# Gated attention followed by a Hyena-style gate: six PSUM banks become one pool, and score runs take two or three units

## The chip, the cores and the metric

The kernel runs on one core of one Trainium2 chip. The metric is the time on the device in microseconds (us), the median of several executions. Besides, one execution is recorded by the hardware profiler; its trace gives the start and duration of each instruction and what each engine waited for. Below, PE is TensorE (matmuls), PEld its weight loads, ACT is ScalarE, DVE is VectorE, POOL is GpSimd and SP is SyncE, which issues most DMAs.

## The reference, cut to what matters

```python
B, S, D = 8, 3136, 256          # d_qk = 64
scores = (z @ z.transpose(0, 2, 1)) / S
attn   = np.maximum(scores, 0.0) ** 2
x      = u * (attn @ v)                       # gated attention
proj   = x @ w_proj                           # D -> 3 D
x1, x2, x3 = proj[..., :D], proj[..., D:2*D], proj[..., 2*D:]
X2 = np.fft.rfft(x2, n=S, axis=1)
H  = np.fft.rfft(filter_fft, n=S, axis=0)[None]
y  = x1 * np.fft.irfft(X2 * H, n=S, axis=1) * x3
out = y @ w_out
```

The inputs and the output are float32. The matmuls run in bfloat16 and accumulate in float32.

## The kernel before, in words

**Scores and weighing.** A batch entry has 3136 positions, cut into 25 tiles of 128 (the last has 64 rows) on one side and into seven chunks of 512, 512, 512, 512, 512, 256 and 320 columns on the other. A *unit* is a chunk with two tiles (with up to four of a narrow chunk). For each unit PE multiplies z with itself: matmuls of 64 rows (line 1352), two at a time, one in the upper and one in the lower half of the array, since d_qk is 64. Their result fills a pair of PSUM banks. ACT takes the relu of the pair (line 1527, tile R), DVE or ACT squares it (1536 or 1534, tile A, eight buffers), and PE weighs v with it (1382, all 128 rows), adding up in two further banks, one for each half of D (`ps_o`). As scores are symmetric, part of the units is not computed again: a DMA transpose (1467) mirrors A tiles into M tiles, which are weighed for later chunks. The last, 64-row tile is weighed separately (1489, `weigh_short`), tacked on to a later score group, `DELAY` groups on. When a chunk is complete, DVE multiplies with u (1577, two results xT).

**All the rest.** From xT PE computes the three projections (901, 913, 946), and a discrete Fourier transform in two steps of small matmuls forwards (758, then 819 and 811), the product with the filter on DVE (1019), and the same backwards (827 and 811, then 1109), then the output matmul (1140). Each of these writes one PSUM bank, which ACT or DVE evicts. Intermediate spectra go through DRAM.

**The order** is made while the program is built. A planner (class `Plan`) holds tasks with an assumed cost on each engine and due times of DMAs, keeps a queue for each kind of PE task and lists for the other engines, and fixes each engine's instruction order. On PE the kinds are S (scores), W (weighing), and FA, FB, FZ (the rest). S comes first whenever it can start within 0.04 us. Whether W or the others come next is set by a credit, which grows by `PACE` with every W and falls with the cost of the others. A task is ready when its inputs and its buffers (`takes`, classes `Slots`) are. The planner adds 0.11 us whenever PE changes between S and any other kind. `Plan.pick` gives a task that both ACT and DVE can do to the second one if it would be done earlier there. On the chip the engines follow the fixed order and wait on semaphores.

**PSUM** has eight banks in the kernel before:

```python
ps_s = Pool("ps_s", 2, [P, 2, 512], F32, PS)          # two pairs, for scores
ps_o = [Pool(f"ps_o{dh}", 1, [P, 512], F32, PS) for dh in range(2)]
ps_m = Pool("ps_m", 2, [P, 512], F32, PS)             # all other matmuls
groups = [scored[i : i + 2] for i in range(0, len(scored), 2)]
```

An S task is a group of two units and takes both pairs of `ps_s`. When no W is left, at the end of the kernel, other matmuls may also use a bank of each `ps_s` pair and the `ps_o` banks (`Plan.choice`, `plan.spare`).

Of the kernel before, what the change touches and what calls it, by code (L numbers as in the profile page):

```python
# [25 lines left out]
HOLD = 3  # L26
DELAY = 2
LATE_PUT, LATE_LOAD, LATE_TURN, LATE_C, LATE_D2 = 3.0, 1.0, 1.5, 2.5, 1.0
# [3 lines left out]
FINAL = (0, 2, 4, 6, 1, 3, 5)  # L32
ZP, ZL = 0, 0.0
REACH = 2
INF = float("inf")
# [7 lines left out]
def c_dve(n):  # L43
    return 0.068 + n * 0.00104
# [14 lines left out]
class Slots:  # L59
# [4 lines left out]

    def take(self):
        self.taken += 1
        self.freed.append(None)
        return self.taken - 1

    def when(self, ahead=0):  # L70
        i = self.taken + ahead - self.n
        if i < 0:
            return 0.0
        if i >= len(self.freed) or self.freed[i] is None:
            return INF
        return self.freed[i]


# [23 lines left out]
class Plan:  # L102


    def __init__(self):
        self.free = {e: 0.0 for e in ("PE", "ACT", "DVE", "SP", "POOL")}
        self.queues = {"S": [], "W": [], "FA": [], "FB": [], "FZ": []}
        self.pend = {e: [] for e in ("ACT", "DVE", "SP", "POOL")}
        self.credit = 0.0
        self.mode = None  # L110
        self.n = 0
        self.spare = []
        self.bus = 0.0

# [30 lines left out]
    def run(self, task, engine, start):  # L145
        takes = [self.choice(s) for s in task.takes]
        self.bank = takes[0] if takes else None
        task.slots = [(s, s.take()) for s in takes]
# [12 lines left out]
        for t, i in task.frees:  # L161
            s, k = t.slots[i]
            if i == 0 and getattr(t, "holders", 1) > 1:
                t.holders -= 1
                t.held_to = max(getattr(t, "held_to", 0.0), end + lat)
                continue
            s.freed[k] = max(getattr(t, "held_to", 0.0), end + lat) if i == 0 else end + lat
        for kid in task.kids:
            for d, extra in kid.deps:
                if d is task:  # L170
                    kid.ready = max(kid.ready, end if extra == ISSUED else end + lat + (extra or 0.0))
            kid.left -= 1
            if not kid.left and kid.kind is None:
                self.offer(kid)

    def pick_pe(self):
        t = self.free["PE"]
        got = {}
        for k, window in (("S", 1), ("W", 1), ("FA", 6), ("FB", 6), ("FZ", 6)):
            best = None  # L180
            for task in self.queues[k][:window]:
                s = max(t, self.ready_at(task))
                if s < INF and (best is None or s < best[0] - 1e-9):
                    best = (s, task)
            if best:
                got[k] = best
        if not got:
            return None
        near = t + 0.04
# [56 lines left out]
def kernel(  # L246
# [85 lines left out]
    o_p = Pool("ost", 2, [P, 4, D], F32)  # L332
    ps_s = Pool("ps_s", 2, [P, 2, 512], F32, PS)
    ps_o = [Pool(f"ps_o{dh}", 1, [P, 512], F32, PS) for dh in range(2)]
    ps_m = Pool("ps_m", 2, [P, 512], F32, PS)

    plan.spare = [ps_m.slots, ps_s.slots, *(p.slots for p in ps_o)]

    def bank(dtype=F32):
        if plan.bank is ps_s.slots:  # L340
            return ps_s.tile()[:, 0, :]
        for p in ps_o:
            if plan.bank is p.slots:
                return p.tile()
        return ps_m.tile([P, 512], F32) if dtype == F32 else ps_m.tile([P, 1024], BF16)

# [5 lines left out]
    def pe(kind, emit, cost, deps=(), takes=(), **kw):  # L352
        return job(kind, lambda e: emit(), {"PE": cost}, deps, takes, **kw)
# [169 lines left out]
    for i, (t0, t1) in enumerate(zip(z_cuts, z_cuts[1:])):  # L523
        step_ = -(-(t1 - t0) // -(-(t1 - t0) // 8))
        for g0 in range(t0, t1, step_):
# [31 lines left out]

            tt = pe("FA", turn, c_pe(*[P] * nt), [(c0, 0.22), (c1, 0.22)], takes=[ps_m.slots])
            tt.frees.append((c0, 0))
# [108 lines left out]

    t4_t = pe("FB", t4_pe, 0.06, [t1_done], takes=[ps_m.slots])
    t4_done = on("DVE", t4_copy, 0.35, [t4_t])  # L670
# [42 lines left out]
    for i0 in range(0, NS, 8):  # L713
# [11 lines left out]

        tt = pe("FB", turn, c_pe(*[P] * n), [s2_done[-1]], takes=[ps_m.slots])
        tb = job(None, back, {"DVE": c_dve2(n * KR)}, [tt], prio=3)
# [23 lines left out]
    def dft1(kind, get, t0, nt, dst, deps, free=None, late=0.0):  # L751
# [14 lines left out]

        a = pe(kind, mm, c_pe(n), deps, [ps_m.slots, s1_p.slots])
        if free:
# [92 lines left out]
    for j0 in range(0, NJ, 4):  # L861
        ld, ibox = load_spec(DF, j0, 4, puts, LATE_F)
        for i in range(4):
# [9 lines left out]

            a = pe("FB", mm, c_line(j0 + i), [*s2_done, ld], [ps_m.slots])
            if i == 3:
# [9 lines left out]
    def add_proj(b, c, xt, xt_tasks):  # L885
# [7 lines left out]
        def to_gates():  # L893
            for nb in range(2):
# [27 lines left out]

                a = pe(kind, mm1, c_pe(cw, cw), xt_tasks, [ps_m.slots, x1_p.slots])
# [4 lines left out]
                a3 = pe(kind, mm3, c_pe(cw, cw), [*xt_tasks, a], [ps_m.slots, g_p.slots])  # L928
                e3 = on("DVE", ev3, c_dve(cw), [a3, e1], prio=late)
# [4 lines left out]
        def to_spectrum():  # L934
            t0, n = T0[c], len(tiles[c])
            at = 0
            while at < n:
# [15 lines left out]

                a = pe("FA", mm2, c_pe(*[D] * (2 * nt)), xt_tasks, [ps_m.slots, x2_p.slots])
                e2 = job(None, ev2, both(nt * D), [a])
# [18 lines left out]
    def add_spectrum(b, puts):  # L974
# [7 lines left out]
        for g in range(NJ // 2):  # L982
# [9 lines left out]
            for i in range(2):  # L992
# [12 lines left out]

                a = pe("FB", mm, c_line(j), [ld, *deps0, *firsts], [ps_m.slots, *([] if i else [xh.slots])])
                firsts = [a]
# [23 lines left out]
            def inv(g=g, xb=xb, z_=z_, a0=a0, gh=gh):  # L1031
# [3 lines left out]
                for i in range(2):  # L1035
# [17 lines left out]
                    a = pe(  # L1053
                        "FB", mm, c_line(j) * (1 + final), [z_, *gx["firsts"], *(minus_task if final else [])], [ps_m.slots] + ([gh.slots] if new else [])
                    )
# [29 lines left out]
    def add_end(b, lasts, gtasks, cs, kind="FB", src=c_p, dsts=(o_p,), late=0, behind=(), then=(), split=False, mids=(y_p,)):  # L1085
        for at, c in enumerate(cs):
# [7 lines left out]
            for dh in range(2):  # L1094
# [16 lines left out]
                def ev(dh=dh, c=c, w=w, box=box, yb=yb):  # L1111
# [3 lines left out]
                    kind, mm, c_pe(*[P] * nt), [ld, t4_done, *firsts, gtasks[2 * c + dh][1], *then],  # L1115
                    [ps_m.slots] + ([mid.slots] if dh == 0 else []),
                )
# [10 lines left out]
            for i0 in range(0, nt, 2):  # L1128
# [16 lines left out]
                def eo(e, i0=i0, n=n, last=last, box=box, ob=ob):  # L1145
# [9 lines left out]
                    kind, mo, c_pe(*[D] * (2 * n)), [*ys, *firsts],  # L1155
                    [ps_m.slots] + ([dst.slots] if i0 == 0 else []),
                )
# [184 lines left out]

    def score_mm(un):
        b, c, k = un
        cw = CHUNKS[c]
        ps = ps_s.tile()
        zt = zT[b]
# [43 lines left out]
    def add_weigh(un, data, done):  # L1391
        global_k = len(plans[un[:2]])

        def part(dhs):
            b, c, k = un
            cw = CHUNKS[c]
            n = sum(t < NT - 1 for t in plans[b, c][k][1])
# [3 lines left out]
                [ps_o[dh].slots for dh in dhs] if k == 0 else [],  # L1401
            )
            if b == 0 and c == 0:
                after(t, next(at for n_, at in V_AT if max(plans[b, c][k][1]) < n_))
# [71 lines left out]

    ends_at = {}
    for gi, g in enumerate(groups):
# [15 lines left out]
    for gi, g in enumerate(groups):  # L1494
# [12 lines left out]
        def sg(g=g, more=more):  # L1507
            for un in g:
                score_mm(un)
# [6 lines left out]
        tails[gi] = st  # L1516
        for i, un in enumerate(g):
            b, c, k = un
# [43 lines left out]
            if last:  # L1562
# [3 lines left out]
                for dh in range(2):  # L1566

                    def xe(dh=dh, b=b, c=c, cw=cw, xt=xt):
# [102 lines left out]
```

## Time and profile before

| | |
|---|---|
| median of 3 executions | 1018.22 us (1015.94 to 1019.5) |
| the profiled execution | 1017.51 us, of it the span from first to last instruction 1015.7 us |
| granted clock of TensorE, mean | 0.995 |
| busy: PE, ACT, DVE, POOL | 97%, 88%, 80%, 18% of the span |
| matmuls | 6046 |
| units scored (relu instructions, line 1527) | 528 |
| HBM read and written | 141 GB/s over the span |

A line of a group in the profile gives line, engine, operation, output and inputs by the program's names, shapes and count, then busy time and mean duration, then the engine's idle time just before. A line of the timeline gives start (us), duration (us), engine, line and operation, and in brackets an idle time before it. A line of the waits gives who waited for whom, total us, number of times and the longest. "issue" stands for time in which the engine waited for nothing that the profile shows. Matmuls overlap, so their durations add up to more than the time they take; the distance from start to start is the cost of one.

### The profile page before, as it was taken

How to read it: one execution, taken by the hardware profiler on the slowest of the kernel's cores; microseconds unless marked ns; L12 is line 12 of the kernel's file. 1: busy time of each engine (PE TensorE's matmuls, PEld its weight loads, DVE VectorE, ACT ScalarE, POOL GpSimd, SP SyncE). 2: the span in 40 equal slices, each digit the busy share in tenths (PEclk: the TensorE clock that was granted, in tenths of full speed). 3: DMA queues.
4: the chain of work that ended last, by engine and by line, in shares of the span. 5: the costliest groups of instructions: out<-in, count | busy, mean ns of one | idle time of the engine just before them, and what ended most of it. 6: DMA issues, size and time to landing. Idle time of an engine off the chain costs nothing.

```text
span 1015.7 us, 17732 instructions
## 1 busy us (share of the span) xinstructions
PE 989.6 (97%) x6046; PEld 483.1 (48%) x6046; DVE 812.8 (80%) x1469; ACT 892.0 (88%) x1218; POOL 186.7 (18%) x401
## 2 busy tenths in 40 slices
PE   6999999999999999999999999999999999999986
PEld 2344544455444554446444464444644455444664
DVE  7866688978889688987789778887798868896574
ACT  5988899988999799897999979998899979998774
POOL 5042301121012210213012131113201221000000
PEclk9999999999999999999999999999999999999989
DMA  9799769878986998898978779896899779968456
GB/s 166 135 172 171 143 128 176 164 145 172 210 176 126 164 205 192 153 158 149 226 159 151 142 159 217 159 177 141 167 208 175 148 137 198 215 145 170 110 184 208
DMA packets 331770, 170.18 MB, mean 168 GB/s; under 512 B 241160, under 2 KB 306504, under 8 KB 331680
## 3 DMA queue, kind: packets, MB, share of 16 engines
q1 hardware_dynamic: 303952, 138.09, 62.5%
q0 software_dynamic: 27728, 30.97, 21.0%
q8 instruction: 47, 0.77, 0.3%
q14 instruction: 43, 0.35, 0.1%
HBM read 90.26 MB, written 53.35 MB: 141 GB/s over the span
## 4 chain that ended last, share of the span: by engine, by line
PE 91%; DVE 4%; ACT 1%; issue 1%; DMA 1%; SPq 1%; ACTq 0%; DVEq 0%
PE ps_o_t L1382 48%; PE ps_s_t L1352 13%; PE ps_m_t L946 5%; PE ps_m_t L913 4%; PE ps_m_t L901 4%; PE ps_m_t L1140 4%; PE ps_m_t L758 3%; PE ps_m_t L819 3%; PE ps_m_t L827 3%; PE ps_m_t L1109 2%; PE ps_o_t L1489 1%; ACT R_t L1527 1%; DVE xT_t L1577 1%; PE ps_m_t L811 1%; DVE yT_t L1112 1%
## 5 line engine op out<-in xcount | busy, mean ns | idle before, releaser
L1527 ACT ACTIVATE R_t<-ps_s_t 128x1024 f32<-128x1024 f32 (+3 forms) x528 | 474.6, 939 | 40.9 <-PE ps_s_t L1352 30.5
L1382 PE MATMUL ps_o_t<-A_t,v_t 128*128 128x512 bf16 (+2 forms) x2016 | 458.3, 355 | 1.3 <-DMA un_t<-in_u_dram 0.7
L1382 PEld LDWEIGHTS <-v_t 128*128 128x128 bf16 x2688 | 254.0, 98 | 227.0 <-issue 27.5
L1536 DVE TENSOR_TENSOR A_t<-R_t 128x1024 bf16<-128x1024 f32 (+2 forms) x269 | 297.0, 1111 | 31.3 <-ACT R_t L1527 23.0
L1534 ACT ACTIVATE A_t<-R_t 128x1024 bf16<-128x1024 f32 (+4 forms) x259 | 247.9, 967 | 5.3 <-DMA M_t<-A_t 1.6
L1352 PE MATMUL ps_s_t<-zT_t 64*128 64x512 bf16 (+2 forms) x1064 | 153.8, 357 | 1.7 <-ACT R_t L1527 1.2
L410 POOL COPY tick<-xT_t 1x1 bf16<-1x1 bf16 x54 | 11.7, 217 | 731.9 <-DVE xT_t L1577 731.9
L1577 DVE SCALAR_TENSOR_TENSOR xT_t<-ps_o_t,uT_t 128x256 bf16<-128x256 f32 (+2 forms) x224 | 76.2, 382 | 35.6 <-PE ps_o_t L1382 29.9
L921 DVE TENSOR_TENSOR gate_t<-ps_m_t,x_t 128x256 bf16<-128x256 f32 (+2 forms) x208 | 68.9, 384 | 35.9 <-PE ps_m_t L913 22.2
L361 ACT ACTIVATE x_t<-ps_m_t 128x512 bf16<-128x512 f32 (+2 forms) x115 | 63.4, 573 | 24.9 <-PE ps_m_t L901 21.3
L1019 DVE TENSOR_TENSOR xh<-xh,H 100x1024 bf16<-100x1024 bf16 x120 | 81.1, 684 | 4.6 <-ACT xh L361 3.9
L1382 PE MATMUL ps_o_t<-M_t,v_t 128*128 128x512 bf16 (+2 forms) x352 | 82.0, 353 | 0.0
L1352 PEld LDWEIGHTS <-zT_t 64*128 64x128 bf16 x1064 | 34.4, 94 | 99.4 <-issue 96.8
L365 DVE CAST x_t<-ps_m_t 128x512 bf16<-128x512 f32 (+2 forms) x92 | 57.1, 636 | 12.8 <-PE ps_m_t L946 8.8
L1112 DVE TENSOR_TENSOR yT_t<-ps_m_t,gate_t 128x512 bf16<-128x512 f32 (+2 forms) x95 | 57.2, 617 | 12.3 <-PE ps_m_t L1109 11.1
L365 DVE CAST s_t<-ps_m_t 128x512 bf16<-128x512 f32 (+1 forms) x65 | 43.0, 668 | 23.4 <-PE ps_m_t L758 22.9
L401 POOL DMA_DIRECT2D un_t<-in_u_dram x112 | 59.9, 556 | 6.8 <-issue 5.5
L420 POOL DMA_DIRECT2D v_t<-in_v_dram x112 | 59.6, 554 | 5.7 <-issue 3.1
L946 PE MATMUL ps_m_t<-wp,xT_t 128*128 128x256 bf16 x394 | 57.4, 273 | 0.7 <-DVE gate_t L921 0.5
L901 PE MATMUL ps_m_t<-xT_t,wp 128*128 128x512 bf16 (+2 forms) x210 | 54.6, 355 | 1.5 <-DVE xT_t L1577 1.4
L1140 PE MATMUL ps_m_t<-wo,yT_t 128*128 128x256 bf16 (+1 forms) x344 | 52.4, 274 | 1.9 <-DVE yT_t L1112 1.6
L913 PE MATMUL ps_m_t<-xT_t,wp 128*128 128x512 bf16 (+2 forms) x208 | 52.7, 355 | 0.1
(196 smaller groups left out, 958.4 us busy)
## 6 DMA issues: line engine op xcount, KB each, us to landing
out_dram<-ost_t SPq DMA_DIRECT2D x66, 256.0 KB
spec<-s_t SPq DMA_DIRECT2D x96, 128.0 KB
spec_in_t<-spec SPq DMA_DIRECT2D x28, 392.0 KB
spec<-gs_t SPq DMA_DIRECT2D x28, 392.0 KB
v_t<-in_v_dram POOLq DMA_DIRECT2D x80, 128.0 KB, 3.7
un_t<-in_u_dram POOLq DMA_DIRECT2D x80, 128.0 KB, 4.8
conv_in_t<-spec SPq DMA_DIRECT2D x33, 256.0 KB
out_dram<-ost_t SPq DMA_DIRECT2D x19, 128.0 KB
```

The costliest lines, as they stand in the source:

```text
L365: nc.vector.tensor_copy(out_, in_)
L901: nc.tensor.matmul(box["p"][:, :cw], wp16[:, k, ds(nb * P, P)], xt["t"][:, k, :cw], start=(k == 0), stop=(k == 1),)
L913: nc.tensor.matmul(box["p3"][:, :cw], wp16[:, k, ds((4 + nb) * P, P)], xt["t"][:, k, :cw], start=(k == 0), stop=(k == 1),)
L946: nc.tensor.matmul(box["p"][:, ds(k_ * D, D)], xt["t"][:, k, ds((at + k_) * P, P)], wp16[:, k, ds(D, D)], start=(k == 0), stop=(k == 1),)
L1019: nc.vector.tensor_tensor(x[:, 1 - i], x[:, 0], h, ALU.mult)
L1140: nc.tensor.matmul(box["p"][:rows, ds(i * D, D)], yb["y"][:, k, ds((i0 + i) * P, rows)], wo16[:, k, :], start=(k == 0), stop=(k == 1),)
L1352: nc.tensor.matmul(blocks(ps, len(pair), cw)[:m, i], zt[h, ds(t * P, m)], zt[h, ds(C0[c], cw)], start=True, stop=True)
L1382: nc.tensor.matmul(o, row(v16[b], t)[:, ds(dh * P, P)], x, start=(k == 0 and i == 0), stop=(last and i == len(pair) - 1),)
L1527: nc.scalar.activation(blocks(box["R"], n, cw)[:rows], blocks(live[un], n, cw)[:rows], AF.Relu)
L1534: nc.scalar.activation(a, r, AF.Square)
L1536: nc.vector.tensor_tensor(a, r, r, ALU.mult)
L1577: nc.vector.scalar_tensor_tensor(x, f, inv_s2, ut, ALU.mult, ALU.mult)
```

## The change

The pools `ps_s` and `ps_m` become one store of six banks, three tiles of two banks each. `Pairs` gives out a whole tile to a score unit, and `Singles` one bank to any other matmul; a single is put beside one that is held longest, and at most `MOST = 3` singles are held at once. An S task is one unit (`GROUP = 1`). The planner decides when a run of S tasks starts: with more than `AMPLE` us of weighing queued (`backlog`) it wants three free pairs, otherwise two; until they are free, other tasks that can start earlier go first, the F kinds only with more than `BACKLOG` us queued. A run that has begun goes on as long as a pair is free within `STAY` us. Further: the F kinds go ahead of W only when less than `FULL` us of work is queued on ACT and DVE; the second engine is charged (`YIELD`) for tasks that only it can do and that would be held up; `DELAY` goes from 2 groups of two to 4 groups of one; and the second xT evaluation counts as ready when the first is issued, not when it has ended.

```diff
-DELAY = 2
+DELAY = 4
+GROUP = 1
+BACKLOG, AMPLE, STAY = 2.0, 4.0, 0.1
+MOST = 3
+FULL = 3.0
+YIELD = 1.0
...
+class Pairs:
+    def when(self, ahead=0):
+        return sorted(max(x) for x in self.banks.at)[ahead]
+    def take(self, now=0.0):
+        k = min(range(len(self.banks.at)), key=lambda i: max(self.banks.at[i]))
+        self.banks.at[k] = [INF, INF]
+        return k
...
+class Singles:
+    def when(self, ahead=0):
+        held = sorted(self.ends.values(), reverse=True)
+        room = held[MOST - 1] if len(held) >= MOST else 0.0
+        return max(room, sorted(t for x in self.banks.at for t in x)[ahead])
+    def take(self, now=0.0):
+        at = self.banks.at
+        free = [(i, h) for i in range(len(at)) for h in range(2)]
+        k = min(free, key=lambda k: (max(at[k[0]][k[1]], now), -at[k[0]][1 - k[1]], k))
...
     def pick_pe(self):
+        more = self.queues["S"]
+        if more and not more[0].left:
+            left = self.backlog()
+            if self.mode == "S":
+                if "S" in got and got["S"][0] <= t + STAY:
+                    return (*got["S"], "S")
+                got.pop("S", None)
+            else:
+                want = 3 if left > AMPLE else 2
+                free = self.pairs.when(min(want, len(more)) - 1)
+                if "S" in got and free > t + 0.04:
+                    rest = {k: v for k, v in got.items() if k != "S" and (k == "W" or left > BACKLOG)}
+                    if rest and min(v[0] for v in rest.values()) < free:
+                        got = rest
+                    elif free < INF:
+                        return max(got["S"][0], free), got["S"][1], "S"
...
-        order += ["FA", "FB", "W", "FZ"] if self.credit > 0 else ["W", "FA", "FB", "FZ"]
+        order += ["FA", "FB", "W", "FZ"] if self.credit > 0 and self.queued(t) < FULL else ["W", "FA", "FB", "FZ"]
...
     def pick(self, e):
-                if s + task.cost[e] >= max(self.free[first], task.ready) + behind + task.cost[first]:
+                end = s + task.cost[e]
+                held = max((end - max(x.ready, s) for x in self.pend[e] if len(x.cost) == 1 and x.ready < end), default=0.0)
+                if end + YIELD * held >= max(self.free[first], task.ready) + behind + task.cost[first]:
...
-    ps_s = Pool("ps_s", 2, [P, 2, 512], F32, PS)
+    ps_t = [ps_p.tile([P, 2, 512], F32, name=f"ps_s{i}") for i in range(3)]
+    banks = Banks(3)
+    pair_slots, one_slots = Pairs(banks), Singles(banks)
-    ps_m = Pool("ps_m", 2, [P, 512], F32, PS)
-    plan.spare = [ps_m.slots, ps_s.slots, *(p.slots for p in ps_o)]
+    plan.spare = [one_slots, *(p.slots for p in ps_o)]
...
-    groups = [scored[i : i + 2] for i in range(0, len(scored), 2)]
+    groups = [scored[i : i + GROUP] for i in range(0, len(scored), GROUP)]
...
-        st = pe("S", sg, sum(costs) + extra, deps, [ps_s.slots] * len(g))
+        st = pe("S", sg, sum(costs) + extra, deps, [pair_slots] * len(g))
...
-                        "DVE", xe, c_dve(cw), [w_last[dh], u_tasks[b, c], *evs], [xT_p.slots] if dh == 0 else [], prio=-1
+                        "DVE", xe, c_dve(cw), [w_last[dh], u_tasks[b, c], *((d, ISSUED) for d in evs)], [xT_p.slots] if dh == 0 else [], prio=-1
```

All other uses of `ps_m.slots` as a task's bank become `one_slots`, with no further change.

More of the change, by code (lines that the diff above doesn't have):

```diff
@@ L76, in when, with __init__, settle, __setitem__ @@
         return self.freed[i]
+class Banks:
+    def __init__(self, pairs):
+        self.at = [[0.0, 0.0] for _ in range(pairs)]
+    def settle(self, k, t):
+        self.at[k[0]][k[1]] = t
+class Pairs:
+    def __init__(self, banks):
+        self.banks, self.freed = banks, self
+    def when(self, ahead=0):
[4 more added lines that the diff above has]
+        return k
+    def __setitem__(self, k, t):
+        self.banks.at[k] = [t, t]
+class Singles:
+    def __init__(self, banks):
+        self.banks, self.freed, self.ends = banks, self, {}
+    def when(self, ahead=0):
+        held = sorted(self.ends.values(), reverse=True)
+        room = held[MOST - 1] if len(held) >= MOST else 0.0
+        return max(room, sorted(t for x in self.banks.at for t in x)[ahead])
+    def take(self, now=0.0):
+        at = self.banks.at
+        free = [(i, h) for i in range(len(at)) for h in range(2)]
+        k = min(free, key=lambda k: (max(at[k[0]][k[1]], now), -at[k[0]][1 - k[1]], k))
+        at[k[0]][k[1]] = INF
+        self.ends = {x: t for x, t in self.ends.items() if t > now}
+        self.ends[k] = INF
+        return k
+    def __setitem__(self, k, t):
+        self.banks.settle(k, t)
+        self.ends[k] = t
 class Task:
@@ L112, in __init__ @@
         self.spare = []
+        self.pairs = None
         self.bus = 0.0
@@ L147, in run @@
         self.bank = takes[0] if takes else None
-        task.slots = [(s, s.take()) for s in takes]
+        task.slots = self.got = [(s, s.take(start)) for s in takes]
         cost = task.cost[engine]
@@ L174, in run, with backlog, queued @@
                 self.offer(kid)
+    def backlog(self):
+        left = 0.0
+        for w in self.queues["W"]:
+            if w.source is not None and w.source.end is None:
+                break
+            left += w.cost["PE"]
+        return left
+    def queued(self, t):
+        some = {id(x): x for e in ("ACT", "DVE") for x in self.pend[e] if x.ready <= t + 0.3}
+        return sum(max(0.0, self.free[e] - t) for e in ("ACT", "DVE")) + sum(min(x.cost.values()) for x in some.values())
     def pick_pe(self):
@@ L188, in pick_pe @@
             return None
+        more = self.queues["S"]
[14 more added lines that the diff above has]
+                        return max(got["S"][0], free), got["S"][1], "S"
+            if not got:
+                return None
         near = t + 0.04
         order = ["S"]
-        order += ["FA", "FB", "W", "FZ"] if self.credit > 0 else ["W", "FA", "FB", "FZ"]
+        order += ["FA", "FB", "W", "FZ"] if self.credit > 0 and self.queued(t) < FULL else ["W", "FA", "FB", "FZ"]
         for k in order:
@@ L332 @@
     o_p = Pool("ost", 2, [P, 4, D], F32)
-    ps_s = Pool("ps_s", 2, [P, 2, 512], F32, PS)
+    ps_p = ctx.enter_context(tc.tile_pool(name="ps_s", bufs=1, space=PS))
+    ps_t = [ps_p.tile([P, 2, 512], F32, name=f"ps_s{i}") for i in range(3)]
+    banks = Banks(3)
+    pair_slots, one_slots = Pairs(banks), Singles(banks)
     ps_o = [Pool(f"ps_o{dh}", 1, [P, 512], F32, PS) for dh in range(2)]
-    ps_m = Pool("ps_m", 2, [P, 512], F32, PS)
-    plan.spare = [ps_m.slots, ps_s.slots, *(p.slots for p in ps_o)]
+    plan.pairs = pair_slots
+    plan.spare = [one_slots, *(p.slots for p in ps_o)]
     def bank(dtype=F32):
-        if plan.bank is ps_s.slots:
-            return ps_s.tile()[:, 0, :]
         for p in ps_o:
@@ L344, in bank @@
                 return p.tile()
-        return ps_m.tile([P, 512], F32) if dtype == F32 else ps_m.tile([P, 1024], BF16)
+        i, h = plan.got[0][1]
+        x = ps_t[i][:, h, :]
+        return x if dtype == F32 else x.bitcast(dtype)
     def job(kind, emit, cost, deps=(), takes=(), **kw):
@@ L556, in turn @@
                     )
-            tt = pe("FA", turn, c_pe(*[P] * nt), [(c0, 0.22), (c1, 0.22)], takes=[ps_m.slots])
+            tt = pe("FA", turn, c_pe(*[P] * nt), [(c0, 0.22), (c1, 0.22)], takes=[one_slots])
             tt.frees.append((c0, 0))
@@ L667, in t4_copy @@
         nc.vector.tensor_copy(T4[:, P : P + N1], box1["p"][:, 0:N1])
-    t4_t = pe("FB", t4_pe, 0.06, [t1_done], takes=[ps_m.slots])
+    t4_t = pe("FB", t4_pe, 0.06, [t1_done], takes=[one_slots])
     t4_done = on("DVE", t4_copy, 0.35, [t4_t])
@@ L724, in back @@
             copy(e, TZ[:KC, ds(i0, n), 0:KR], src)
-        tt = pe("FB", turn, c_pe(*[P] * n), [s2_done[-1]], takes=[ps_m.slots])
+        tt = pe("FB", turn, c_pe(*[P] * n), [s2_done[-1]], takes=[one_slots])
         tb = job(None, back, {"DVE": c_dve2(n * KR)}, [tt], prio=3)
@@ L1053, in inv @@
                     a = pe(
-                        "FB", mm, c_line(j) * (1 + final), [z_, *gx["firsts"], *(minus_task if final else [])], [ps_m.slots] + ([gh.slots] if new else [])
+                        "FB", mm, c_line(j) * (1 + final), [z_, *gx["firsts"], *(minus_task if final else [])], [one_slots] + ([gh.slots] if new else [])
                     )
@@ L1341, in blocks, with score_mm @@
         return x[:].rearrange("p i j -> p (i j)")[:, 0 : n * cw].rearrange("p (i j) -> p i j", i=n)
-    def score_mm(un):
+    def score_mm(un, where):
         b, c, k = un
         cw = CHUNKS[c]
-        ps = ps_s.tile()
+        ps = ps_t[where]
         zt = zT[b]
@@ L1395, in part @@
             b, c, k = un
+            src = None if plans[b, c][k][0] == "M" else scored_by[un]
             cw = CHUNKS[c]
@@ L1402, in part @@
             )
+            t.source = src
             if b == 0 and c == 0:
@@ L1475, in mirror @@
             t_.frees.append((q_, 0))
-    ends_at = {}
+    ends_at, scored_by = {}, {}
     for gi, g in enumerate(groups):
@@ L1507, in sg @@
         def sg(g=g, more=more):
-            for un in g:
-                score_mm(un)
+            for un, (_, where) in zip(g, plan.got):
+                score_mm(un, where)
             for x in more:
@@ L1514 @@
         extra = sum(c_pe(CHUNKS[c]) for _, c in more)
-        st = pe("S", sg, sum(costs) + extra, deps, [ps_s.slots] * len(g))
+        st = pe("S", sg, sum(costs) + extra, deps, [pair_slots] * len(g))
         tails[gi] = st
+        scored_by.update({un: st for un in g})
         for i, un in enumerate(g):
```

17 lines of the change are left out of this document (8 added, 9 removed).

## The prediction

> **What bounds the kernel now.** I read the page first: the engines' busy shares and the chain of work that ended last.
>
> ```profile
> span 1015.7 us, 17732 instructions
> PE 989.6 (97%) x6046; PEld 483.1 (48%) x6046; DVE 812.8 (80%) x1469; ACT 892.0 (88%) x1218; POOL 186.7 (18%) x401
> ...
> PE 91%; DVE 4%; ACT 1%; issue 1%; DMA 1%; SPq 1%; ACTq 0%; DVEq 0%
> PE ps_o_t L1382 48%; PE ps_s_t L1352 13%; PE ps_m_t L946 5%; PE ps_m_t L913 4%; PE ps_m_t L901 4%; PE ps_m_t L1140 4%; PE ps_m_t L758 3%; PE ps_m_t L819 3%; PE ps_m_t L827 3%; PE ps_m_t L1109 2%; PE ps_o_t L1489 1%; ACT R_t L1527 1%; DVE xT_t L1577 1%; PE ps_m_t L811 1%; DVE yT_t L1112 1%
> ```
>
> TensorE (PE) carries 91% of the chain, so time is won or lost in its own stream. Next the waits: does PE wait for anybody?
>
> ```profile
> PEld L1352 <- issue: 96.8, 266, 0.8
> ACT R_t L1527 <- PE ps_s_t L1352: 30.5, 61, 1.8
> DVE xT_t L1577 <- PE ps_o_t L1382: 29.9, 30, 3.4
> ...
> PE ps_s_t L1352 <- ACT R_t L1527: 1.2, 3, 0.5
> ```
>
> The columns are total us, times, longest. ACT and DVE wait for PE's results (30 us each in these two rows); PE waits for ACT's relu of a score bank three times, 1.2 us. What repeats is the first row: 266 times the weight load of a score run (264 of them) stands alone. The timeline of PE shows what such a run costs:
>
> ```profile
> 519.49 1.03 PE L1382 MATMUL ps_o_t<-A_t,v_t 128*128 128x512 bf16 x4
> 520.38 0.67 PE L819 MATMUL ps_m_t<-spec_in_t,S 98*100 98x512 bf16 x2
> 520.90 1.03 PE L1382 MATMUL ps_o_t<-A_t,v_t 128*128 128x512 bf16 x4
> 521.86 0.60 PE L1352 MATMUL ps_s_t<-zT_t 64*128 64x512 bf16 x4
> 522.39 0.42 PE L819 MATMUL ps_m_t<-spec_in_t,S 98*100 98x512 bf16 x1
> 522.64 1.03 PE L1382 MATMUL ps_o_t<-A_t,v_t 128*128 128x512 bf16 x4
> 523.51 0.38 PE L819 MATMUL ps_m_t<-spec_in_t,S 98*100 98x512 bf16 x1
> ```
>
> Read starts, not durations, because neighbours overlap. Four 512-column matmuls take 0.87 us from start to start when another 128-row matmul follows (522.64 to 523.51), and 0.96 us when a score run follows (520.90 to 521.86): entering costs 0.09 us. The run's four 64-row matmuls go two at a time, so they stream like two (2 x 0.216 = 0.43 us); the next group starts 0.53 us after the run: leaving costs 0.10 us.
>
> Over all records I worked out the same from start times. A 512-column matmul is followed by another 128-row one after 216 ns (median) and by a score run after 312 ns; the last pair of a run is followed after 308 ns instead of 213. So **one score run costs 0.096 + 0.095, about 0.19 us, whatever its length**; 264 runs make 50.5 us. Inside a run the second pair starts 223 ns after the first: no such charge. The whole span is then: streaming 918 us, run charges 50.5 us, some 33 us of other stalls (about 10 in the first 50 us, 12 after 955 us, 11 scattered between), and 13.5 us before the first and after the last matmul's start.
>
> **The change, part by part.**
>
> *Runs two or three units long.* There are 528 scored units (x528 of the relu line) in 264 runs of two. With n runs the charge is 0.191 n. All runs of two: no gain. All of three: 176 runs, 88 x 0.191 = 16.8 us less. Which share? The new rule asks for three free pairs only where more than 4.0 us of weighing is queued, for two below that. From the matmuls' order I summed, at the start of each run between 50 and 950 us, the score columns not yet weighed: 2.8 us at the 5th percentile, 4.3 in the median, 6.0 at the 95th, and over 4.0 in 56% of the runs; mirrored tiles add to the new count, so three are wanted in perhaps 60%. But three pairs are all six banks, so no other matmul's bank may be in use then. There are some 880 single-bank uses, each held about 1.35 us (median 1.14 us from its last matmul's start to the end of its eviction, and its matmuls before): 880 x 1.35 = 1190 us, or 1.2 banks held on average; at only some 15% of the present run starts is none held. The planner may fill with weighing until they drain, and an alternation of two weighings and one other task leaves such moments, so I put three at half of the runs, between the 60% that want it and what the held banks allow: mean 2.5 units, 211 runs, 53 x 0.191 = **10.1 us less**. Bounds: 0 and 16.8 us; below nothing if runs of one appear, at 0.191 us for each additional run.
>
> *Other matmuls share the six banks, at most three at once.* Before they had two of their own. Three instead of two would release PE where it stalls on evictions, but the rows show no such stall beyond parts of the 11 us in the middle; I take no gain. The cost is on the other side: a score run now needs banks that ACT's relus and, new, ACT's and DVE's evictions of singles must leave. Behind a waiting score matmul stands all of PE: the queue is in order, so weighing whose data are ready waits too, and behind it ACT and DVE. Today a run starts 0.49 us (median) after the last relu's end, 0.16 us at the 10th percentile, so it hardly ever waits. The nearest row for a late one is the 1.2 us above (3 waits, 0.4 us each). I take 0.01 us per run, twice what those 1.2 us make over 264 runs, **2 us more**; from 0 to 0.1 us for every run, 21 us, if the cover, evictions that are done by then, is gone.
>
> *DELAY 2 to 4 with GROUP 2 to 1.* The short tile's weighing was put two groups of two later and is now four units later: the same distance. It is the same 112 matmuls of line 1489 in the same 64-row mode. They now need their square four units before in time; that can cut a run short in at most 56 places. Half of them at 0.19 us would be 5 us, but at least four units (over 7 us of PE at 3.85 us per run of two) lie between, against some 4 us for relu, square and their queues; I take 0 to 1 us, taken as 0.5.
>
> *FULL, YIELD, and the second xT evaluation that waits for issue only.* These alter the order on PE, ACT and DVE, not the instructions. DVE (80%) and ACT (88%) have idle time of 203 and 124 us, and both results of xT come from DVE in order anyway. Zero, between -2 and +3 us: an order that is worse for ACT shows up as PE's waits, priced above.
>
> *Head and tail.* After the last chunk, singles could use two banks of their own, one in each of two score tiles and two accumulators, six; now three plus two accumulators, five. The tail waits for DVE, not for banks:
>
> ```profile
> 983.59 0.27 PE L811 MATMUL ps_o_t<-xh,zT_t 100*98 100x256 bf16 x1
> 983.70 0.38 PE L811 MATMUL ps_o_t<-xh,TZ 100*98 100x256 bf16 x2
> 984.13 0.31 PE L811 MATMUL ps_s_t<-R_t,TZ 100*98 100x256 bf16 x1
> 985.34 0.37 PE L811 MATMUL ps_s_t<-R_t,zT_t 100*98 100x256 bf16 x1 [0.89 <-DVE R_t L1019]
> ...
> 986.14 0.42 PE L811 MATMUL ps_m_t<-xh,zT_t 100*98 100x256 bf16 x1
> ```
>
> These stand in the timeline of PE, and the stall of 0.89 us is followed by a stretch at half clock: 256-column matmuls step by 0.11 us before and 0.21 us after it, until about 992 us; the granted clock is 0.91 from 960 us on against 1.00 before. Half speed over 7 us costs 3.5 us. One bank less can add a stall or lengthen that stretch; another order can remove it. I take 1 us more, between -4 and +4.
>
> Sum: -10.1 + 2 + 0.5 + 0 + 1 = **-6.6 us**. The profiled execution took 1017.5 us (span 1015.7 and 1.8 around it), 0.7 us under the median of three, 1018.2. So 1010.9 profiled, and **1012 us** as a median (1011.6 rounded).
>
> **The Trainium skill against the rows.** "Perfetto Trace Analysis", section Identifying the Most-Contended Engine, says that matmul occupancy is a bad measure of TensorE and that the weight loads' busy share should be read instead, occupancy for the others. Here that is 48% for weight loads against 88% for ACT, and by that rule ACT, not PE, would be the engine to relieve and the change would be worth nothing. The start times above and the waits of ACT on PE speak against it in this trace. "TensorEngine Tiling (Array Packing)", section Key Properties, says that a change of tiling mode drains TensorE; the charge of 0.19 us per run is the same thing with its price here.
>
> **The rivals.**
>
> 1. *Score runs wait for evictions, slower.* For: a run now waits for up to three relus and three evictions on two engines, one of them 88% busy; the planner reckons a 1024-element relu at 0.91 us and a square on DVE at 1.13 where the rows by form have 1.03 and 1.22 us, so banks come free later than planned. Against: today's plan has the same optimism and PE's waits are 1.2 us. Price: with 211 runs the 10.1 us less the 1.5 us of head, tail and DELAY are gone at 0.04 us per run; from there on this decides. At 0.1 us it is 21 - 8.6 = +12.5, **1031 us**; at 0.06 us, 1022.
> 2. *No longer runs.* Singles are always in flight, the third pair hardly ever comes free, runs stay at two: 264 charges, and small costs and gains cancel: **1018 us**. For: a bank was held at 85% of the starts. Against: the planner is free to wait.
> 3. *ACT is the bound.* It is busy 892 us; were PE's saved time only lent, its idle time would fill and the end stay: 1018 us. Against: ACT's largest idle row waits for PE's scores.
> 4. *Nearly all runs are of three.* 176 to 185 runs, 15 to 17 us less, with 1 us of waits: **1002 us**. For: 56% of the starts had the backlog. Against: the held banks.
>
> **How the numbers follow.** Forecast (between 1004 and 1015): 0.50. Rival 4: 0.14. Rival 2: 0.09; rival 3: 0.03. Rival 1: 0.24. A measurement of this kernel tells about 0.3%, 3 us, from no change. Faster by more: 0.50 + 0.14 = 0.64. Within: 0.12. Slower: 0.24. The range takes the forecast, rivals 2 and 3, most of rival 4 (down to 1000) and rival 1 up to 0.09 us per run (19 - 8.6 = +10, 1028): 1000 to 1028. The forecast's own range is 1004 to 1015.
>
> **What would show it.** Score runs: 200 to 240 groups of L1352, with x6 in the timeline where three units go together; the issue row before L1352's weight loads falls from 96.8 us by the ratio of the runs (to some 80). PE's wait on score banks stays under 5 us. If it is 20 us or more, rival 1 holds; if there are over 255 runs, rival 2; if ACT's idle time nears nothing while PE's gaps grow, rival 3. I am wrong in the mechanism if the runs fall by 50 and the time doesn't follow.

## The result, and the profile after

The changed kernel took 1126.51 us (median of 5, 1125.9 to 1128.39) against 1018.22 before: ratio 1.106, 95% interval 1.105 to 1.108. The forecast was 1012, the range 1000 to 1028: far outside, and on the other side. The same lines of the page and of the waits, after (line 1446 is the score matmul that was 1352, 1476 the weighing, 1624 the relu, 1633 the square on DVE; all lines have moved by about 94):

```profile
span 1125.1 us, 17563 instructions
...
PE 1002.1 (89%) x5952; PEld 498.6 (44%) x6046; DVE 833.3 (74%) x1440; ACT 896.4 (80%) x1247; POOL 188.7 (17%) x401
...
PE 50%; ACT 20%; DVE 19%; issue 7%; DMA 2%; SPq 0%; DVEq 0%; ACTq 0%; another core or an unknown queue 0%
```

```profile
PEld L1446 <- issue: 90.3, 239, 1.1
...
ACT R_t L1624 <- PE ps_s L1446: 53.5, 67, 5.2
...
ACT x_t L455 <- DVE x_t L459: 13.9, 20, 1.7
...
ACT x_t L455 <- DVE gate_t L1015: 12.0, 15, 1.8
...
PE ps_s L1007 <- DVE gate_t L1015: 6.9, 10, 1.2
```

All engines are busy about as long as before and idle longer, and the chain, 91% PE before, now goes from engine to engine. The telling rows are the last three. An eviction on ACT (x_t, line 455) waits for an eviction on DVE, and a projection on PE (1007) for an eviction that has nothing to do with it. Among the longest waits of the kernel before, no eviction on ACT waits for one on DVE.

Taken apart as in the prediction, from the starts of all matmuls (some 95 of 6046 records are missing after; their streaming time is put back): 201 score runs instead of 264, which is 12.0 us less charge, and 156 us of PE stalls instead of 33, **123 us more**. Of the 156 us, some 127 lie between two matmuls of 128 rows, where there were 29 before. Entering a score run costs no more than it did; the rest of the increase lies inside score runs and right behind them.

The timeline of the kernel after shows one such place:

```profile
74.41 0.59 PE L1007 MATMUL ps_s<-xT_t,wp 128*128 128x512 bf16 x2
...
74.61 0.60 ACT L455 ACTIVATE x_t<-ps_s 128x512 bf16<-128x512 f32 x1
...
75.24 0.69 DVE L459 CAST x_t<-ps_s 128x512 bf16<-128x512 f32 x1 [0.60 <-ACT x_t L455]
75.85 0.75 DVE L1015 TENSOR_TENSOR gate_t<-ps_s,x_t 128x256 bf16<-128x256 f32 x2
...
76.65 0.59 PE L1007 MATMUL ps_s<-xT_t,wp 128*128 128x512 bf16 x2 [1.21 <-DVE gate_t L1015]
```

DVE's cast starts 0.03 us after ACT's eviction has ended, though it reads the other bank of the same tile. The next pair of projection matmuls (76.65) then waits 1.21 us for the gate's multiplication, which reads the bank beside the one that it writes. The semaphore waits in the built program say why. Before, each single bank was a tile of its own. Now two tasks can have the two halves of one tile, `ps_t[i][:, h, :]`, and the program's dependencies are drawn for the tile as a whole, readers against readers included. Of the waits among PE, ACT and DVE that stand on a matmul or an eviction itself (further ones stand on weight loads and on separate wait instructions and aren't counted here), 839 are for an instruction that uses only the *other half* of the tile: 416 of PE for an eviction, 265 of an eviction for a matmul, 158 between ACT and DVE. In 26 of the 839 the two instructions also share an SBUF buffer. In the kernel before there is none. The planner, which reckons each half by itself, knows nothing of them.

### The profile page after: what moved, and what is told of

It is laid out like the page before. It is cut to its first block, busy times and chain, and to the rows that moved or that the text cites. A ratio compares the mean times of both kernels' runs of the same rounds, so it can differ in the third digit from the quotient of the medians.

```text
span 1125.1 us, 17563 instructions
## 1 busy us (share of the span) xinstructions
PE 1002.1 (89%) x5952; PEld 498.6 (44%) x6046; DVE 833.3 (74%) x1440; ACT 896.4 (80%) x1247; POOL 188.7 (17%) x401
## 4 chain that ended last, share of the span: by engine, by line
PE 50%; ACT 20%; DVE 19%; issue 7%; DMA 2%; SPq 0%; DVEq 0%; ACTq 0%; another core or an unknown queue 0%
PE ps_o_t L1476 24%; PE ps_s L1446 7%; ACT R_t L1624 6%; DVE A_t L1633 4%; PE ps_s L1040 3%; ACT x_t L455 3%; DVE gate_t L1015 3%; PE ps_s L1234 3%; PE ps_s L995 3%; PE ps_s L1007 2%; DVE x_t L459 2%; ACT xh L455 2%; ACT s_t L455 2%; DVE yT_t L1206 2%; PE ps_s L913 2%
## 5 line engine op out<-in xcount | busy, mean ns | idle before, releaser
L1624 ACT ACTIVATE R_t<-ps_s 128x1024 f32<-128x1024 f32 (+3 forms) x528 | 471.3, 928 | 75.3 <-PE ps_s L1446 53.5
L1633 DVE TENSOR_TENSOR A_t<-R_t 128x1024 bf16<-128x1024 f32 (+3 forms) x334 | 366.4, 1113 | 114.0 <-ACT R_t L1624 113.0
L1631 ACT ACTIVATE A_t<-R_t 128x1024 bf16<-128x1024 f32 (+4 forms) x194 | 183.1, 948 | 2.5
L1446 PE MATMUL ps_s<-zT_t 64*128 64x512 bf16 (+2 forms) x1064 | 155.6, 357 | 8.1 <-ACT x_t L455 3.1
L455 ACT ACTIVATE x_t<-ps_s 128x512 bf16<-128x512 f32 (+2 forms) x148 | 79.5, 562 | 60.7 <-DVE x_t L459 13.9
L1015 DVE TENSOR_TENSOR gate_t<-ps_s,x_t 128x256 bf16<-128x256 f32 (+2 forms) x214 | 71.8, 384 | 36.9 <-PE ps_s L1007 12.9
L1446 PEld LDWEIGHTS <-zT_t 64*128 64x128 bf16 x1064 | 45.9, 94 | 109.0 <-issue 90.3
L1206 DVE TENSOR_TENSOR yT_t<-ps_s,gate_t 128x512 bf16<-128x512 f32 (+2 forms) x97 | 58.6, 626 | 23.6 <-PE ps_s L1203 8.3
L1007 PE MATMUL ps_s<-xT_t,wp 128*128 128x512 bf16 (+2 forms) x205 | 54.1, 350 | 12.9 <-DVE gate_t L1015 6.9
L1234 PE MATMUL ps_s<-wo,yT_t 128*128 128x256 bf16 (+1 forms) x366 | 53.6, 272 | 13.2 <-ACT ost_t L455 3.6
L1040 PE MATMUL ps_s<-wp,xT_t 128*128 128x256 bf16 x398 | 56.1, 272 | 8.2 <-DVE gate_t L1015 3.5
L995 PE MATMUL ps_s<-xT_t,wp 128*128 128x512 bf16 (+2 forms) x206 | 51.6, 351 | 7.4 <-DVE gate_t L1015 1.8
```

The lines of the kernel that those rows point to most:

```text
L455: nc.scalar.activation(out_, in_, AF.Copy)
L995: nc.tensor.matmul(box["p"][:, :cw], wp16[:, k, ds(nb * P, P)], xt["t"][:, k, :cw], start=(k == 0), stop=(k == 1),)
L1015: nc.vector.tensor_tensor(g[:, ::-1] if h == 0 else g, p, x, ALU.mult)
L1040: nc.tensor.matmul(box["p"][:, ds(k_ * D, D)], xt["t"][:, k, ds((at + k_) * P, P)], wp16[:, k, ds(D, D)], start=(k == 0), stop=(k == 1),)
L1206: nc.vector.tensor_tensor(yb["y"][:, dh, 0:w], box["p"][:, 0:w], gates[b, c, dh][:, 0:w], ALU.mult)
L1234: nc.tensor.matmul(box["p"][:rows, ds(i * D, D)], yb["y"][:, k, ds((i0 + i) * P, rows)], wo16[:, k, :], start=(k == 0), stop=(k == 1),)
```

## The experiments

Theory A: these waits are the loss. Theory B: the true evictions come late (rival 1 of the prediction). Theory C: the new rules of order are bad by themselves. Later ones are D (the length of runs is worth nothing), E (waiting for the third pair starves the others), and F and G (the further rules FULL, YIELD and the later xT cost time, or make room for the long runs).

| kernel | us | ratio to before (95%) | score runs | charge | PE stalls |
|---|---|---|---|---|---|
| before | 1018.2 | | 264 | 50 | 33 |
| after | 1126.5 | 1.1064 (1.1049 to 1.1079) | 201 | 38 | 156 |
| own_banks | 1011.9 | 0.9930 (0.9912 to 0.9948) | 201 | 38 | 39 |
| before_shared | 1178.2 | 1.1560 (1.1543 to 1.1578) | 264 | 50 | 196 |
| before_shared_own | 1018.8 | 0.9993 (0.9978 to 1.0008) | 264 | 50 | 35 |
| own_banks_evictions | 1083.7 | 1.0635 (1.0615 to 1.0655) | 201 | 38 | 113 |
| own_banks_matmuls | 1033.9 | 1.0150 (1.0128 to 1.0172) | 201 | 38 | 62 |
| rules_only | 1044.1 | 1.0260 (1.0235 to 1.0284) | 272 | 52 | 59 |
| own_banks_no_rules | 1044.7 | 1.0267 (1.0241 to 1.0294) | 205 | 39 | 72 |
| own_banks_two | 1021.4 | 1.0035 (1.0023 to 1.0047) | 227 | 43 | 44 |
| own_banks_three | 1115.4 | 1.0954 (1.0939 to 1.0969) | 187 | 36 | 146 |
| own_banks_costs | 1064.9 | 1.0463 (1.0447 to 1.0478) | 212 | 40 | 93 |
| own_banks_tuned | 1007.3 | 0.9893 (0.9870 to 0.9916) | 202 | 39 | 32 |

Charge is 0.191 us times the runs, stalls are all else that lies between matmuls' starts beyond streaming, both in us and worked out as above. Stalls thus hold the time at a lower clock too: the mean granted clock of the profiles is 0.995 or more, but 0.991 in rules_only and own_banks_no_rules, 0.989 in own_banks_three and 0.986 in own_banks_costs. Against 0.995, the missing share of these spans makes some 4 to 10 us, an estimate. The ratios are to runs of the kernel before on the same chip.

**own_banks.** After the planner has emitted everything, the dependencies are drawn anew: those on the same bank are stated one by one, those between the two halves are taken out. The order on every engine is that of the changed kernel, instruction by instruction. In the cut, `use` holds the (tile, half) that an instruction uses, and `keep` the instructions that also share SBUF data with it.

```diff
     plan.go()
+    by_bank(tc, ps_t, ("PE", "rest"))
...
+            for k in use:
+                if e == engines["PE"]:
+                    for r in readers.get(k, []):
+                        tc.add_manual_dep(x, r.name, info, reason="bank free")
+                    writer[k], readers[k] = x, []
+                else:
+                    tc.add_manual_dep(x, writer[k].name, info, reason="bank full")
+                    readers[k].append(x)
...
+            tc.add_to_no_dep_group(f"bank{i}_{h}_{e}", x)
+            for f in engines.values():
+                pair = "PE" if engines["PE"] in (e, f) else "rest"
+                if f != e and pair in what:
+                    tc.declare_no_dep(x, group=f"bank{i}_{1 - h}_{f}", keep=list(keep.values()), reason="another bank")
```

> The changed kernel, its instruction order kept, but each half of a pair has its own dependencies: waits of an instruction for one that uses only the other half are taken out, those for the same bank stay. Theory A (false waits between the halves of a pair are the loss): 1005 to 1015 us, PE's stalls outside the score runs back from some 140 to under 45 us. Theory B (the true evictions come late, rival 1 of the prediction): 1090 us or more, since they still come as late. Theory C (the new rules of order are bad): 1090 us or more as well.

1011.85 us, within A's range, some 80 us below what B and C expected. Of the 839 waits 16 are left, in all of which the two share an SBUF buffer. In its timeline the same piece of work (lines 1059 and 1067 here are 1007 and 1015 there, 507 and 511 the evictions) runs thus:

```profile
69.52 0.59 PE L1059 MATMUL ps_s<-xT_t,wp 128*128 128x512 bf16 x2
69.54 0.58 ACT L507 ACTIVATE x_t<-ps_s 128x512 bf16<-128x512 f32 x1
69.72 0.69 DVE L511 CAST x_t<-ps_s 128x512 bf16<-128x512 f32 x1
...
70.33 1.44 DVE L1067 TENSOR_TENSOR gate_t<-ps_s,x_t 128x256 bf16<-128x256 f32 x4
70.38 0.59 PE L1059 MATMUL ps_s<-xT_t,wp 128*128 128x512 bf16 x2
```

ACT and DVE evict side by side, and PE's second projection starts while the gate is being read; no bracket of idle time is left on these rows. The two evictions take 0.58 and 0.69 us, as long as one after the other above.

**before_shared** and **before_shared_own.** The kernel before, where nothing of the rules, the runs or the order is changed; only its two single banks become halves of one tile, and in the second the halves get their own dependencies again.

```diff
-    ps_m = Pool("ps_m", 2, [P, 512], F32, PS)
+    ps_m = Pool("ps_m", 1, [P, 2, 512], F32, PS)
+    ps_m.slots = Slots(2)
+    both_m = ps_m.tile()
...
-        return ps_m.tile([P, 512], F32) if dtype == F32 else ps_m.tile([P, 1024], BF16)
+        x = both_m[:, (ps_m.slots.taken - 1) % 2, :]
+        return x if dtype == F32 else x.bitcast(dtype)
```

> The kernel before, order and all else kept, but its two single banks are the halves of one tile instead of two tiles. Theory A: it loses about as much as the change did, 1070 to 1130 us, with ACT and DVE waiting for each other's evictions. Theories B and C: unchanged, 1016 to 1020 us, since nothing is later or in another order.

> The kernel before with its two single banks as halves of one tile (1178.2 us), and each half given its own dependencies. Theory A: back to the kernel before, 1016 to 1022 us, since only the waits for the other half differ. If taking out those waits by declaration brings something of its own, it ends elsewhere.

1178.2 us, 160 us lost by an edit of a few lines, more than A expected (1070 to 1130). The likely reason is that with only two single banks every neighbour shares the tile (944 waits for the other half, counted as above, against 839 in the changed kernel). And back to 1018.8 us with dependencies by half, so taking waits out brings nothing of its own. In the waits of PE of before_shared the pattern of the changed kernel is plain:

```profile
PE ps_m_t L949 <- DVE gate_t L924: 11.5, 20, 1.4
PE ps_m_t L916 <- ACT x_t L364: 8.9, 21, 0.7
PE ps_m_t L1112 <- DVE yT_t L1115: 7.7, 21, 0.6
```

Matmuls of projections and inverse transforms wait for evictions of the neighbouring half. This settles A against B and C: the same order without the waits is fast, and the old order with them is slow.

**own_banks_evictions** and **own_banks_matmuls.** The changed kernel with only one kind of these waits taken out: `by_bank(tc, ps_t, ("rest",))` between ACT and DVE, and `by_bank(tc, ps_t, ("PE",))` between PE and an eviction.

> The changed kernel with only the waits between ACT and DVE for the other half taken out; PE still waits for evictions of the other half and evictions for matmuls into it. Theory A: part of the loss, 1050 to 1100 us. Theories B and C: within 10 us of 1126.

> The changed kernel with only the waits between PE and an eviction of the other half taken out; ACT and DVE still wait for each other's evictions in one pair. Theory A: the larger part of the loss goes, since PE is what the time hangs on: 1020 to 1060 us. Theories B and C: within 10 us of 1126.

Both as A expected. The waits that PE takes part in are worth 92.6 us (1126.5 to 1033.9), those between ACT and DVE 42.8; together 114.7, less than their sum, probably since a late eviction on ACT or DVE costs mostly through the PE that waits for it; that was not separated.

**rules_only.** All the new rules of order (GROUP, DELAY, the rule that starts a run, FULL, YIELD and the later xT), with PSUM divided as before.

```diff
-    ps_t = [ps_p.tile([P, 2, 512], F32, name=f"ps_s{i}") for i in range(3)]
-    banks = Banks(3)
-    pair_slots, one_slots = Pairs(banks), Singles(banks)
+    ps_t = [ps_p.tile([P, 2, 512], F32, name=f"ps_s{i}") for i in range(2)]
+    banks = Banks(2)
+    pair_slots = Pairs(banks)
...
+    ps_m = Pool("ps_m", 2, [P, 512], F32, PS)
+    one_slots = ps_m.slots
...
-                want = 3 if left > AMPLE else 2
+                want = 2
```

> The changed rules of order (GROUP 1, DELAY 4, FULL, YIELD, the later xT), but PSUM divided as before: two pairs for scores, two single banks. No two tasks share a tile. 272 score runs instead of 264. Theory A: 1014 to 1024 us (8 more runs at 0.19 us are 1.5 us). Theory C (the rules of order are bad by themselves): 1060 us or more.

1044.05 us, 2.6% more, between the expectations of A and C: the rules alone cost 26 us of stalls and 8 runs. About half of the additional stalls lie after 955 us (24 us against 12). So with PSUM divided as before C holds in part, but not for the 108 us. Which of the rules does it was not separated.

**own_banks_no_rules.** The counterpart: pool, runs and DELAY with a half's own dependencies, without FULL, YIELD and the later xT.

```diff
-FULL = 3.0
-YIELD = 1.0
+FULL = 1e9
+YIELD = 0.0
...
-    ... [w_last[dh], u_tasks[b, c], *((d, ISSUED) for d in evs)], ...
+    ... [w_last[dh], u_tasks[b, c], *evs], ...
```

> The kernel with a half's own dependencies (1011.9 us), without FULL, YIELD and the later xT: only the pool, the runs and DELAY are left. 205 score runs instead of 201. Theory F (the three further rules cost the 26 us that the changed rules lost with PSUM divided as before): 1000 to 1010 us. Theory G (they make room for the long runs: without them ACT and DVE are late with evictions and squares): 1020 to 1035 us.

1044.7 us, 33 us more than with the rules. F (1000 to 1010) is out; the direction is G's, the size above its range (1020 to 1035). With the pool, FULL, YIELD and the later xT together carry the gain. By the page ACT is busier without them and DVE idler (own_banks above, of which some matmul records are missing; no rules below):

```profile
PE 968.9 (96%) x5949; PEld 487.5 (48%) x6046; DVE 820.5 (81%) x1440; ACT 881.7 (87%) x1247; POOL 188.0 (19%) x401
```

```profile
PE 992.3 (95%) x6046; PEld 490.0 (47%) x6046; DVE 778.9 (74%) x1412; ACT 926.8 (89%) x1275; POOL 189.3 (18%) x401
```

42 us less work on DVE stand against 45 us more on ACT, which has the relus to do; DVE's squares wait 153.5 us for them instead of 109.4. Which of the three rules does it was not separated.

**own_banks_two** and **own_banks_three.** `AMPLE = 1e9` (two pairs are always enough) and `AMPLE = 0.0` (always three), with a half's own dependencies.

> The kernel with a half's own dependencies (1011.9 us), but a run never waits for a third pair: 227 runs instead of 201. Theory A with the charge of 0.19 us per run: 26 x 0.19 = 5 us more, 1016 to 1018. Theory D (the length of runs is worth nothing, the gain is from the third single bank): 1010 to 1013.

> The same, but a run always wants three free pairs: 187 runs. Theory A: 14 x 0.19 = 2.7 us less, 1008 to 1010, if waiting for the third pair costs nothing. Theory E (the wait for the third pair starves ACT or the weighing): 1013 us or more. Theory D: 1010 to 1013.

Two: 9.6 us more than own_banks, of it 5.0 us of charge, as A reckoned, and 5 us of stalls that neither theory had. 1021.4 us lies above A's range (1016 to 1018) and well above D's (1010 to 1013): D is out, but as the order changes too, the price of the charge alone isn't isolated. Three: 104 us more although the charge falls by 2.7 us; E holds, and far beyond what I thought. The waits of own_banks_three and then of own_banks name the place:

```profile
DVE A_t L1685 <- ACT R_t L1676: 212.1, 143, 3.9
...
ACT R_t L1676 <- PE ps_s L1498: 98.7, 98, 6.6
...
PE ps_o_t L1528 <- DVE A_t L1685: 35.1, 67, 1.2
```

```profile
DVE A_t L1685 <- ACT R_t L1676: 109.4, 103, 2.7
...
ACT R_t L1676 <- PE ps_s L1498: 55.9, 84, 5.2
```

Scores come so late that ACT waits for them, DVE's squares for ACT, and weighing, which should fill the wait, for the squares (35.1 us; in own_banks the same row of PE's waits is 2.7 us). Waiting for the third pair is free only as long as weighing is in store.

**own_banks_costs.** The planner reckons with durations near those of the profile.

```diff
-    return 0.055 + n * 0.000833
+    return 0.06 + n * 0.00095
...
-    return 0.068 + n * 0.00104
+    return 0.068 + n * 0.00112
```

> The same as with a half's own dependencies, but the planner reckons ACT at 0.06 + 0.00095 us per element and DVE at 0.068 + 0.00112, near the durations that the profile shows (1.03 and 1.22 us for 1024), instead of 0.91 and 1.13. 212 runs. Theory A: the charge is 2.1 us more, but banks come free when planned, PE's stalls of some 40 us fall by 5 to 15: 1000 to 1009 us. Theory B in its weak form (late evictions still cost some us) says the same; if PE's remaining stalls come from elsewhere: 1012 to 1016.

A miss: 1064.9 us. The new costs change the order throughout. Of the 54 us of additional stalls some 17 lie in the last 75 us. There PE waits once for 6.9 us for a DMA (conv_in_t, line 1255) and ACT, behind PE, once for 10.6 us; the granted clock from 990 to 1030 us is 0.79. Why the truer costs make a worse order elsewhere was not found. Banks planned later did not make PE stall less, which gives B no support.

**own_banks_tuned.** `PACE 0.55, BACKLOG 1.75, STAY 0.15, DELAY 5`, with a half's own dependencies.

> The kernel with a half's own dependencies, and four constants moved: PACE 0.55, BACKLOG 1.75, STAY 0.15, DELAY 5. 202 score runs. The charge of the runs is the same as with 201, so all that it can gain is stalls: 1004 to 1010 us if the planner's shorter order holds on the chip, 1011 to 1016 if not.

1007.33 us, faster than the kernel before by 1.1% (0.8 to 1.3) and than the changed one by 10.6%. The charge is 12 us below that of the kernel before, and the stalls, 32 us, are back where they were.

## Why the prediction was wrong

**The score runs: right.** Forecast were 211 runs and 10.1 us less, measured 201 runs and 12.0 us. In the kernel after, a 512-column matmul is followed by a score run after 311 ns, as before (312), so entering costs what it did. In own_banks_tuned 12 us less charge go with a time that is 11 us shorter; as stalls are what is left of the span, this fits but is no separate proof. The issue row before the score weight loads, by which the prediction would have seen the runs (some 80 us), is no measure of them: 90.3 us in the changed kernel, 37.3 in own_banks, with 201 runs in both.

**The step that failed is "Other matmuls share the six banks".** I put 2 us there, between 0 and 21. All stalls together rose by 123 us, and 117 of them go when the waits between halves are taken out in the same order (156 to 39). The prediction's own sign of a wrong mechanism came true: the runs fell by 63 and the time didn't follow. Two things were wrong in the step. It took each of the six banks to come free by itself, as the planner does; that halves of one tile share their dependencies was in the diff (`ps_t[i][:, h, :]` in place of `ps_m.tile`), and I read it as a mere address. And it looked only at score runs, which wait little, and not at the 880 single-bank uses: spread over 839 waits, 117 us are 0.14 us for each. The rows would have given a bound: an eviction takes 0.6 to 0.7 us, so if each of the 880 uses waited for a neighbour's, that would be some 570 us, an estimate that says only that the term need not be small.

**Rival 1 named the right side by the wrong mechanism.** It had score runs wait for evictions that are late. PE's waits at score matmuls stay small (3.1 us in the largest row, 7 us in all), and the price of 0.04 to 0.1 us per run has nothing to do with what happened: B fell with own_banks and before_shared. Rivals 2 and 3 are out as well: runs are longer, and own_banks is faster with ACT still at 87%. For the rule of the Trainium skill ("Perfetto Trace Analysis", Identifying the Most-Contended Engine) the prediction took only half of what the page names: beside the weight loads' busy share it names MFU, the matmul work as a share of the peak. Read by the weight loads alone, which made ACT the engine to relieve, it is not borne out: they are 48% busy in own_banks as before, and the time is 0.7% shorter (0.5 to 0.9). The prediction's own 918 us of streaming in 1015.7, an estimate in place of MFU, would have put PE ahead of ACT. Rival 4 has a limit that I missed: own_banks_three, with 187 runs and 1115.4 us.

**FULL, YIELD and the later xT: taken as zero, between -2 and +3.** With the pool they are worth -33 us. With PSUM divided as before their worth isn't known: the 26 us of stalls of rules_only are those of all the rules of order together. Saying that they change no instruction was no bound, and not quite true: YIELD decides which engine takes a task, and ACT has 1247 instructions with the three rules (own_banks) and 1275 without. An order is worth more here than the whole gain in charge. That own_banks came out at 1011.85 us, next to the 1012 forecast, is luck in part: the charge fell 2 us further than reckoned and the stalls rose by 6 us where the other terms made 3.5, and the sum rests on these rules working with the pool, which I had not shown.

**DELAY, head and tail** have no measurement of their own; the stalls after 955 us are some 10 us in own_banks and 12 before, so nothing shows that one bank less at the end cost time.

"PSUM — Partial Sum Buffer", section PSUM bank collisions raise a hardware error, of the Trainium skill says that two engines must be kept apart in one bank and quadrant of partitions, and that accesses to different banks may go on together. The runs agree: in own_banks ACT and DVE read the two banks of one tile at once at 69.72 us, and each takes as long as alone. What stood between the halves was the program's bookkeeping, not the chip.

## What to carry to other kernels

Before pooling buffers, ask at what grain the program's dependencies are drawn: two tasks in one tile can wait for each other although the chip would let them run side by side, and a planner that doesn't know it will plan around buffers that are not free. In the profile it shows as evictions on one engine that wait for evictions on another. And going from 128-row to 64-row matmuls and back has a price that can be read off starts, 0.19 us here; longer runs win it back only as long as other work is in store while they are collected.

## What the runs showed that was not expected

Nothing new of the chip itself; what surprised was how sharply the time depends on order and waits. One threshold, AMPLE, between 4.0 and 0 moves it by 104 us, and an edit of a few lines that joins two tiles into one costs 160 us, with every engine's instructions and their order the same.
